# Attention, mixture of experts and feed-forward on one core: the weighted sum of a pair of heads as one group

## The chip, the cores and the metric

The kernel runs on one core of a Trainium2 chip. The metric is the device time of one execution in microseconds. PE is the matrix engine, DVE, ACT and POOL are the vector, scalar and general engines, SP issues most DMAs. PE writes to eight banks of PSUM; DVE and ACT copy from there.

## The reference

Causal attention over 4 batches of 8 heads, 576 queries and keys, head size 64, with a bias from a cumulative sum of `s`; then a top-1 mixture of 8 experts (512 to 1024 to 512) with two gates; then a feed-forward layer 512 to 2048 to 512 with a squared ReLU. Only the attention is touched by the change:

```
scores = scale * np.matmul(q, k.transpose(0, 1, 3, 2))
bias = -(cum[:, :, :, None] - cum[:, :, None, :])
scores = np.where(causal, -1000000000.0, scores + np.minimum(bias, 0.0))
scores = scores - np.max(scores, axis=-1, keepdims=True)
attn = np.exp(scores)
attn = attn / (np.sum(attn, axis=-1, keepdims=True) + 1e-09)
return np.matmul(attn, v)
```

## The kernel before

The attention works on 16 pairs of heads, one pair after the other, and the pairs overlap. The 576 queries are four blocks of 128 and a last one of 64, the last rows. A pair has seven units: blocks 0 and 1 with both heads in one unit, blocks 2 and 3 once for each head (unit 2, 3 and, for the other head, 10, 11), and the last rows of both heads (unit 4). The order within a pair is 0, 1, 3, 11, 2, 10, 4.

For a unit PE computes scores (`emit_s`, L636), DVE adds the mask and takes the row maximum (`emit_m`, L663), ACT takes the exp and its row sum (`emit_e`, L680), PE transposes the result (`emit_t`, L696), and ACT or DVE copies it out (`emit_v`, L715 and L717) into `pt0` (queries of blocks 0 and 1) or `pt1` (the others). From these and v PE makes the weighted sum (`emit_pv`, L733): the first half, 256 queries, in eight rows of the trace, the second half, 320 queries, in twenty. ACT copies it to `oT` (`emit_ov`, L744). PE transposes that back (`emit_xt`, L771), DVE divides by the row sums (`emit_xe`, L806), whose reciprocals are made by `emit_rc` (L759 to L762), and `store_x` sends it to memory. Beside that, q and k of a later pair are transposed by PE (`qk_pe`, L549: four blocks of q, four of k; L551: the last rows of both), split by ACT into a high part (`qk_hi`, L576) and by DVE into a low part (`qk_lo`, L580). For each batch the gate's logits are made from `oT` (`emit_lm`, L828).

The order on each engine is written out by hand: every step is registered by `at(key, function)`, the keys come from the table `K_`, and one sort by key gives the program's order. A pair counts as seven units of key.

PSUM holds three banks "s" for scores, three banks "t" for the transposes of a pair, of q and k, and for the weighted sums, and a pair of banks "s2" for the scores of the last rows. In the banks "t" a pair has thirteen groups: eight of its units (the last rows take two), three of q and k, and the two halves of the weighted sum. The first half of the sum stands early in the next pair's time, the second about five units later.

Of the kernel before, what the change touches and what calls it, by code (L numbers as in the profile page):

```python
# [24 lines left out]
P = 128  # L25
# [17 lines left out]
    lt=[[-0.37, -0.33, 0.07, 0.12], [-0.22, 0.14, 0.64, 0.96]],  # L43
# [12 lines left out]
    qk=[-3.45, -2.16, -1.89],  # L56
    qkh=0.61,
# [3 lines left out]
    pv=[[3.74, 3.87], [8.47, 8.49, 8.51, 8.53, 8.57]],  # L61
# [6 lines left out]
    sx=2.42,  # L68
# [22 lines left out]
def attention_moe_ffn_kernel(  # L91
# [125 lines left out]
    def at(key, fn, *args):  # L217
        tasks.append((key, len(tasks), fn, args))
# [232 lines left out]
    with tc.manual_schedule():  # L451
        with ExitStack() as actx:
# [34 lines left out]
            pt0 = [apool.tile([P, 2, 2, 256], F32, name=f"pt0{a}") for a in range(K_["ptb"])]  # L487
# [13 lines left out]

            raw_q = {}
# [40 lines left out]

            def qk_pe(pp, part):
# [154 lines left out]
            def emit_v(pp, u, act):  # L699
                pb = pp % K_["ptb"]  # L700
                j0 = 0
                for i, (tp, n) in enumerate(t_t.pop((pp, u))):
                    if u < 2:
                        src = tp[:, 0:n * P].rearrange("p (h j i) -> p h j i", h=2, i=P)
                        dst = pt0[pb][:, :, 0:u + 1, u * P:(u + 1) * P]
# [15 lines left out]
            def emit_pv(pp, half, jbs):  # L721
                vt = raw_v[pp]
                if jbs[0] == 0:
                    o_t[pp, half] = ps_o.tile([P, 512], F32, tag=o_tag, name=o_tag)
                o = o_t[pp, half]
                last = 1 if half == 0 else NB - 1
                pt = (pt0 if half == 0 else pt1)[pp % K_["ptb"]]
                n = 256 if half == 0 else S - 256
                base = 0 if half == 0 else 2
                for jb in jbs:  # L730
                    c0 = max(jb - base, 0) * P
                    for hd in range(2):
# [3 lines left out]
                            rhs=pt[:, hd, jb, c0:n],  # L736
# [15 lines left out]
            def emit_rc(pp, half):  # L752
# [4 lines left out]
                b0, b1 = (0, 2) if half == 0 else (2, NB)  # L757
# [476 lines left out]
            order = K_["order"]  # L1234
            NU = len(order)
            at(NU * ND + 0.5, init_spare)

            def early(pp):
                return min(NU, 3 * max(pp - ND, 0))

            for pp in range(NPAIR):
# [5 lines left out]
                if pp >= 1:  # L1247
# [4 lines left out]
                    for part in range(3):  # L1252
                        tq = t0 + K_["qk"][part] - early(pp) + (0 if pp >= ND else K_["q1"])
                        at(tq, qk_pe, pp, part)
                        at(tq + K_["qkh"], qk_hi, pp, part)
                        at(tq + K_["qkl"], qk_lo, pp, part)
                if pp >= ND:
                    tb = t0 + max(K_["dup"], K_["qk"][2] + K_["qkl"] - early(pp) + 0.4)
# [14 lines left out]
                for half in (1, 0) if end else (0, 1):  # L1273
# [5 lines left out]
                    at(tv + K_["rc"], emit_rc, pp, half)  # L1279
# [544 lines left out]
```

## Time and profile before

| what | value |
|---|---|
| median of 3 runs | 861.82 us (861.45 to 862.03) |
| the profiled execution's own time | 862.74 us |
| its span | 861.0 us |
| granted clock of PE in it | 0.998 |
| PE busy | 843.1 us (98%) |
| weight loads of PE busy | 748.7 us (87%) |
| DVE, ACT, POOL busy | 520.4, 452.3, 262.1 us |
| weighted sums (L733) on the chain of waits | 5% of the span |

The span is from the first to the last instruction. Busy time is the union of an engine's instructions, with modelled ends on PE. The chain of waits is followed back from the last instruction, at each step to what released it. The attention takes the first 222 us of the span; the experts and the feed-forward layer, which the change does not touch, follow.

### The profile page before, as it was taken

Reading aid. Unit: us, or ns where it says so; the run is one execution under the profiler, and the core shown is the slowest. Engines: PE = TensorE matmul, PEld = TensorE weight load, DVE = VectorE, ACT = ScalarE, POOL = GpSimd, SP = SyncE. Lnnn points to the kernel's source line nnn. Section 1 sums busy time; section 2 is a strip of 40 time slices with the busy share of each in tenths; the row PEclk is TensorE's granted clock in tenths of the full one; section 3 lists DMA queues with packets and bytes.
Section 4 is the critical chain, followed back from the end, with each engine's and each line's share of the span. In section 5 each row is a group of like instructions: output and inputs, shape, how many; then the busy total and the mean of one; then the engine's idle time right before and its main releaser. Section 6 shows DMA issues by size and latency. Waiting matters only on the chain.

```text
span 861.0 us, 15161 instructions
## 1 busy us (share of the span) xinstructions
PE 843.1 (98%) x5412; PEld 748.7 (87%) x5412; DVE 520.4 (60%) x1180; ACT 452.3 (53%) x1012; POOL 262.1 (30%) x304
## 2 busy tenths in 40 slices
PE   8999999999999999999999999999999999999995
PEld 6876777777799999999999999999999999999994
DVE  7667777978777677768976767664233343232221
ACT  7787878988465446566655545443233232233221
POOL 6322334543126465566422232331101011001001
PEclk9999999999999999999999999999999999999999
DMA  7676677753287898999983433321010121001001
GB/s 168 137 162 142 144 183 180 178 127 91 78 278 232 255 252 266 233 280 274 296 246 96 147 120 101 100 84 62 13 62 37 37 75 38 1 1 37 1 0 40
DMA packets 113029, 113.14 MB, mean 131 GB/s; under 512 B 66034, under 2 KB 83954, under 8 KB 112947
## 3 DMA queue, kind: packets, MB, share of 16 engines
q1 hardware_dynamic: 104962, 96.68, 42.1%
q0 software_dynamic: 3664, 9.62, 3.3%
q10 hardware_dynamic: 4320, 5.80, 2.0%
q8 instruction: 45, 0.74, 0.4%
q14 instruction: 38, 0.30, 0.1%
HBM read 80.50 MB, written 23.32 MB: 121 GB/s over the span
## 4 chain that ended last, share of the span: by engine, by line
PE 47%; issue 31%; DVE 6%; ACT 6%; POOL 5%; DMA 4%; POOLq 1%; SPq 0%; ACTq 0%; DVEq 0%
PE z L1431 14%; PE z L1482 7%; PE z L1473 6%; PE s L636 5%; PE t L733 5%; PE t L696 4%; DMA cv<-in_moe_w_out_dram 2%; ACT p L680 2%; POOL out_dram L1541 1%; DVE w L250 1%; POOL cvm L1400 1%; PE t L549 1%; POOL cvm L1399 1%; ACT sta L576 1%; DMA w_out_d<-cvm 1%
## 5 line engine op out<-in xcount | busy, mean ns | idle before, releaser
L1431 PE MATMUL z<-xt,w 128*128 128x384 f32 (+6 forms) x1920 | 329.7, 320 | 0.7 <-DVE h L1442 0.6
L1431 PEld LDWEIGHTS z<-xt,w 128*128 128x128 f32 x1920 | 308.1, 188 | 9.8 <-DVE h L1442 1.2
L1482 PE MATMUL z<-w,h 128*128 128x512 f32 x864 | 214.9, 393 | 0.0
L1482 PEld LDWEIGHTS z<-w,h 128*128 128x128 f32 x864 | 160.7, 188 | 29.3
L1451 DVE SCALAR_TENSOR_TENSOR r<-z,r 128x384 f32<-128x384 f32 x96 | 53.3, 556 | 127.2 <-ACT r L1450 127.2
L1450 ACT ACTIVATE r<-z 128x384 f32<-128x384 f32 x96 | 47.2, 492 | 150.3 <-PE z L1431 149.3
L1473 PE MATMUL z<-h,w 128*128 128x304 f32 (+5 forms) x768 | 111.3, 294 | 0.4 <-DVE h L1442 0.2
L1473 PEld LDWEIGHTS z<-h,w 128*128 128x128 f32 x768 | 104.0, 189 | 1.2 <-ACT h L1441 0.4
L1399 POOL TENSOR_TENSOR cvm<-cvm,cva 128x512 f32<-128x512 f32 x32 | 43.5, 1361 | 170.6 <-DVE cva L1395 121.9
L1541 POOL DMA_INDIRECT out_dram<-ysb,tok_m x18 | 17.4, 969 | 245.5 <-ACT ysb L1528 183.2
L1458 DVE TENSOR_TENSOR h<-r,h 128x384 fp32r<-128x384 f32 x96 | 61.0, 636 | 50.3 <-ACT h L1457 49.7
L680 ACT ACTIVATE p<-p,nm 128x128 f32<-128x128 f32 (+3 forms) x144 | 84.3, 590 | 3.7 <-DVE nm L663 2.3
L1457 ACT CAST h<-r 128x384 fp32r<-128x384 f32 x96 | 49.3, 513 | 64.1 <-DVE r L1451 63.8
L250 DVE TENSOR_TENSOR w<-stg,w 128x1024 fp32r<-128x1024 f32 x49 | 75.1, 1534 | 5.4 <-ACT w L246 5.4
L663 DVE CUSTOM_DVE_ANT_0 p<-s,mask 128x128 f32<-128x128 f32 (+3 forms) x128 | 59.7, 486 | 30.4 <-PE s L636 29.3
L696 PE MATMUL t<-ident,p 128*128 128x128 f32 x400 | 69.1, 283 | 2.8 <-DVE sta L580 1.1
L246 ACT CAST w<-stg 128x1024 fp32r<-128x1024 f32 x49 | 51.4, 1049 | 22.0 <-POOL cvm L1400 18.2
L696 PEld LDWEIGHTS t<-ident,p 128*128 128x128 f32 x400 | 44.4, 140 | 18.7 <-ACT p L680 6.2
L597 POOL CAST stb<-sta 64x1152 fp32r<-64x1152 f32 x28 | 31.4, 1150 | 79.7 <-PE s L636 46.3
L1400 POOL TENSOR_TENSOR cvm<-cvs,cvm 128x512 f32<-128x512 f32 x32 | 54.2, 1694 | 2.5
L636 PE MATMUL s<-sta 128*64 128x288 f32 (+4 forms) x204 | 50.0, 342 | 0.9 <-DVE sta L580 0.9
L715 ACT COPY pt<-t 128x512 f32<-128x512 f32 (+1 forms) x94 | 47.0, 515 | 7.3 <-PE t L733 4.1
(242 smaller groups left out, 1024.8 us busy)
## 6 DMA issues: line engine op xcount, KB each, us to landing
stg<-in_moe_w_dram SPq DMA_DIRECT2D x42, 512.0 KB
cv<-in_moe_w_out_dram SPq DMA_DIRECT2D x16, 512.0 KB
stx<-in_moe_w_dram SPq DMA_DIRECT2D x14, 512.0 KB
cv<-in_moe_w_in_dram SPq DMA_DIRECT2D x14, 512.0 KB
xr<-yT_d SPq DMA_DIRECT2D x8, 768.0 KB
qk<-in_q_dram SPq DMA_DIRECT2D x32, 128.0 KB
v<-in_v_dram SPq DMA_DIRECT2D x32, 128.0 KB
stg<-in_moe_w_dram SPq DMA_DIRECT2D x16, 256.0 KB
```

Source lines behind the costliest of these rows:

```text
L250: nc.vector.tensor_tensor(out=lo, in0=raw.pop(job), in1=hi.bitcast(F32), op=ALU.subtract)
L636: nc.tensor.matmul(ps[0:mw, d0:d0 + nn], lhsT=ql[r, m0:m0 + mw], rhs=kl[r, c0:c0 + nn], start=(i == 0 and (tail or n == 0)), stop=(done an ...
L663: nc.vector.tensor_tensor_reduce(out=dst, in0=src, in1=msk, scale=-1.0, scalar=3.0e38, op0=ALU.add, op1=ALU.min, accum_out=nm[:, c:c + 1])
L680: nc.scalar.activation(out=pt[:, cs], in_=pt[:, cs], func=AF.Exp, scale=-1.0, bias=nm[:, c:c + 1], accum_out=rs[:, r:r + 1])
L696: nc.tensor.transpose(tp[:, i * P:(i + 1) * P], pt[:, j0:j0 + P], ident)
L1399: nc.gpsimd.tensor_tensor(out=m, in0=m, in1=a.bitcast(F32), op=ALU.mult)
L1400: nc.gpsimd.tensor_tensor(out=m, in0=sq, in1=m, op=ALU.add)
L1431: nc.tensor.matmul(ps[:, 0:n], lhsT=wa[:, zw, kk, fl * P:(fl + 1) * P], rhs=xt[:, zx, kk, 0:n], start=(i == 0), stop=(i == 3 * KD - 1))
L1451: nc.vector.scalar_tensor_tensor(out=gg, in0=ps[:, 0:TT], scalar=0.0, in1=gg, op0=ALU.max, op1=ALU.mult)
L1458: nc.vector.tensor_tensor(out=ht[:, 1], in0=gg, in1=ht[:, 0].bitcast(F32), op=ALU.subtract)
L1473: nc.tensor.matmul(y_acc[g][d][:, 0:n], lhsT=wb[:, zw, fl, d * P:(d + 1) * P], rhs=ht[:, zh, 0:n], start=(f == 0 and i == 0), stop=(f == n ...
L1482: nc.tensor.matmul(acc, lhsT=ht[:, zh, c * P:(c + 1) * P], rhs=wb[:, zw, fl, :], start=(first and i == 0), stop=(last and i == 2))
```

## The change

For pairs 0 to 14 the two halves of the weighted sum stand together, where the second half stood, in one buffer of the bank pair "s2"; ACT copies them out one after the other. The eight transposes of q and k (pairs 2 and 4 to 15; not 3) become one group in another buffer of "s2", behind the scores of the next pair's block 0. The pair of banks has one buffer, so it is used in turn: last rows' scores, q and k, weighted sum, last rows' scores. `pt0` is kept twice, in a layout where each block of keys is contiguous. The reciprocals of both halves are made at once, the first half's division and the store come later. One key moves the first group of logits next to the second. Pair 15 keeps its own arrangement.

```diff
-    lt=[[-0.37, -0.33, 0.07, 0.12], [-0.22, 0.14, 0.64, 0.96]],
+    lt=[[-0.37, -0.33, 0.07, 0.12], [-0.36, 0.14, 0.64, 0.96]],
...
+    qk2=[-2.05, -2.04, -1.59],
+    qkd=[-0.25, 0.54, 0.0],
...
-    pv=[[3.74, 3.87], [8.47, 8.49, 8.51, 8.53, 8.57]],
+    x0=10.87,
+    pv=[[8.45, 8.46], [8.47, 8.49, 8.51, 8.53, 8.57]],
...
-    sx=2.42,
+    sx=3.9,
...
-            pt0 = [apool.tile([P, 2, 2, 256], F32, name=f"pt0{a}") for a in range(K_["ptb"])]
+            pt0 = [apool.tile([P, 2, 3 * P], F32, name=f"pt0{a}") for a in range(2)]
...
+            def in_s2(pp):
+                return pp >= ND and early(pp) != 3
+
             def qk_pe(pp, part):
-                ps = qk_ps[pp, part] = bank(K_["ring"][part])
+                if part < 2 and in_s2(pp):
+                    if part == 0:
+                        qk_ps[pp] = ps_2.tile([P, 1024], F32, tag="s2", name="s2")
+                    ps = qk_ps[pp][:, 512 * part:512 * part + 512]
+                else:
+                    ps = bank(K_["ring"][part])
+                qk_ps[pp, part] = ps
...
                 if jbs[0] == 0:
-                    o_t[pp, half] = ps_o.tile([P, 512], F32, tag=o_tag, name=o_tag)
+                    if pp == NPAIR - 1:
+                        o_t[pp, half] = ps_o.tile([P, 512], F32, tag=o_tag, name=o_tag)
+                    else:
+                        if half == 0:
+                            o_t[pp] = ps_2.tile([P, 1024], F32, tag="s2", name="s2")
+                        o_t[pp, half] = o_t[pp][:, 512 * half:512 * half + 512]
...
                     for part in range(3):
-                        tq = t0 + K_["qk"][part] - early(pp) + (0 if pp >= ND else K_["q1"])
+                        tq = t0 + K_["qk2" if in_s2(pp) else "qk"][part] - early(pp) + (0 if pp >= ND else K_["q1"])
                         at(tq, qk_pe, pp, part)
-                        at(tq + K_["qkh"], qk_hi, pp, part)
-                        at(tq + K_["qkl"], qk_lo, pp, part)
+                        th = K_["qkd"][part] if in_s2(pp) else 0.0
+                        at(tq + th + K_["qkh"], qk_hi, pp, part)
+                        at(tq + th + K_["qkl"], qk_lo, pp, part)
...
-                    at(tv + K_["rc"], emit_rc, pp, half)
+                    if end or half == 1:
+                        at(tv + K_["rc"], emit_rc, pp, half)
+                    if not end and half == 0:
+                        tv = tv - K_["pv"][0][-1] + K_["x0"]
+                        tx = tv + K_["xe"]
                     at(tv + K_["xt"], emit_xt, pp, half)
```

The order of PE from the last rows' scores of one pair to the transposes of its unit 10, in the next pair's time, before (`s_865` is the bank pair, `pt_154` is `pt0`):

```order
L636 MATMUL s_865<-stb_138 128x288 x4
L636 MATMUL s_865<-sta_137 64x288 x4
L549 MATMUL t<-ident,qk 128x128 x4
L733 MATMUL t<-pt_154,v_142 64x256 x2
L733 MATMUL t<-pt_154,v_142 64x128 x2
L696 MATMUL t<-ident,p 128x128 x3
L636 MATMUL s<-sta_135 128x192 x2
L636 MATMUL s<-stb_139 128x192 x2
L549 MATMUL t<-ident,qk 128x128 x4
L771 MATMUL s<-ident,oTx 128x128 x2
L696 MATMUL t<-ident,p 128x128 x3
```

The same stretch of PE in the changed kernel, where lines below L549 are moved by some 17 to 25 (L653 is the scores, L713 the transposes, L566 q and k, L796 the x transposes; `s_901` is the bank pair again):

```order
L653 MATMUL s_854<-stb_138 128x288 x4
L653 MATMUL s_854<-sta_137 64x288 x4
L713 MATMUL t<-ident,p 128x128 x3
L653 MATMUL s<-sta_135 128x192 x2
L653 MATMUL s<-stb_139 128x192 x2
L796 MATMUL s<-ident,oT_310 128x128 x2
L566 MATMUL s_901<-ident,qk 128x128 x8
L713 MATMUL t<-ident,p 128x128 x3
L653 MATMUL s<-sta_135 128x256 x2
```

The first half of the sum (two rows on `pt_154`) is gone from here, q and k have become one row behind block 0's scores and the x transposes, and block 2's transposes follow the last rows' scores at once.

The place of the second half of the sum on PE, before (`pt_155` is `pt1`):

```order
L696 MATMUL t<-ident,p 128x128 x4
L636 MATMUL s<-sta_135 128x384 x2
L733 MATMUL t<-pt_155,v_142 64x320 x6
L733 MATMUL t<-pt_155,v_142 64x192 x2
L733 MATMUL t<-pt_155,v_142 64x64 x2
L696 MATMUL t<-ident,p 128x128 x4
L636 MATMUL s<-stb_139 128x384 x2
```

And in the changed kernel (L758 is the sum, `s_978` the bank pair):

```order
L713 MATMUL t<-ident,p 128x128 x4
L653 MATMUL s<-sta_135 128x384 x2
L758 MATMUL s_978<-pt_154,v_142 64x256 x2
L758 MATMUL s_978<-pt_154,v_142 64x128 x2
L758 MATMUL s_978<-pt_156,v_142 64x320 x6
L758 MATMUL s_978<-pt_156,v_142 64x192 x2
L758 MATMUL s_978<-pt_156,v_142 64x64 x2
L713 MATMUL t<-ident,p 128x128 x4
L653 MATMUL s<-stb_139 128x384 x2
```

Two rows on `pt_154` now stand ahead of those on `pt1`, into the same buffer.

The order of ACT over the same time, from the high part of q to the exps of block 1, before (L744 is the copy of the first half of the sum, L715 copies transposes):

```order
L576 ACTIVATE sta_137<-t 128x512
L744 COPY oTx<-t 128x256
L680 ACTIVATE p,rs_156<-p,nm 128x576
L576 ACTIVATE sta_137<-t 128x512
L715 COPY pt_155<-t 128x3x128
L576 ACTIVATE sta_137<-t 128x2x64
L680 ACTIVATE p,rs_157<-p,nm 128x128 x2
L715 COPY pt_155<-t 128x2x3x64
L715 COPY pt_155<-t 128x2x2x64
L680 ACTIVATE p,rs_157<-p,nm 128x256 x2
```

And in the changed kernel (L697 is the exp, L593 the high parts, L732 the copies, `s_901` is the bank pair):

```order
L697 ACTIVATE p,rs_157<-p,nm 128x576
L593 ACTIVATE sta_137<-s_901 128x512
L732 COPY pt_156<-t 128x3x128
L697 ACTIVATE p,rs_158<-p,nm 128x128 x2
L593 ACTIVATE sta_137<-t 128x2x64
L593 ACTIVATE sta_137<-s_901 128x512
L732 COPY pt_156<-t 128x2x3x64
L732 COPY pt_156<-t 128x2x2x64
L697 ACTIVATE p,rs_158<-p,nm 128x256 x2
```

The exp of the last rows (128x576) now stands first, the copy of the sum is gone, and the high part of k (the second L593 on `s_901`) stands behind block 0's exps and the high part of the last rows.

## Rows read from the trace of the kernel before

**Rows 1.** Chain of waits, the attention: start us, length us, what.

```profile
31.42 2.21 PE t L733 x20
...
45.72 2.21 PE t L733 x20
...
57.75 2.21 PE t L733 x20
69.78 2.21 PE t L733 x20
...
95.94 2.21 PE t L733 x20
108.52 2.21 PE t L733 x20
...
208.66 2.21 PE t L733 x20
```

**Rows 2.** Busy time by stretch: window, us, busy PE PEld DVE ACT POOL, PE clock, DMA, GB/s.

```profile
49.39:190.06 140.67, 138.02 (x1110) 104.32 (x1108) 109.15 (x387) 117.35 (x341) 53.14 (x68) 1.00 0.68 158
```

**Rows 3.** Timeline of PE: start us, us, instruction [idle before <- what ended it].

```profile
61.42 0.78 PE L636 MATMUL s<-stb 128*128 128x288 f32 x4
...
62.56 0.60 PE L549 MATMUL t<-ident,qk 128*128 128x128 f32 x4
63.09 0.87 PE L733 MATMUL t<-pt,v 128*64 128x256 f32 x8
63.89 0.55 PE L696 MATMUL t<-ident,p 128*128 128x128 f32 x3
...
64.71 0.60 PE L549 MATMUL t<-ident,qk 128*128 128x128 f32 x4
65.14 0.38 PE L771 MATMUL s<-ident,oTx 128*128 128x128 f32 x2
...
68.50 0.92 PE L696 MATMUL t<-ident,p 128*128 128x128 f32 x4 [0.15 <-ACT p L680]
```

**Rows 4.** Timeline of ACT, the same lap.

```profile
60.00 0.43 ACT L744 COPY oTx<-t 128x320 f32<-128x320 f32 x1 [1.21 <-PE t L733]
...
63.20 0.60 ACT L576 ACTIVATE sta<-t 128x512 fp32r<-128x512 f32 x1 [0.30 <-PE t L549]
64.01 0.37 ACT L744 COPY oTx<-t 128x256 f32<-128x256 f32 x1 [0.21 <-PE t L733]
64.28 0.78 ACT L680 ACTIVATE p<-p,nm 128x576 f32<-128x576 f32 x1
...
65.39 0.60 ACT L576 ACTIVATE sta<-t 128x512 fp32r<-128x512 f32 x1 [0.24 <-POOL sta L598]
65.89 0.48 ACT L715 COPY pt<-t 128x384 f32<-128x384 f32 x1
...
68.33 0.52 ACT L680 ACTIVATE p<-p,nm 128x256 f32<-128x256 f32 x1
...
68.82 0.72 ACT L680 ACTIVATE p<-p,nm 128x512 f32<-128x512 f32 x1
...
69.53 0.59 ACT L715 COPY pt<-t 128x512 f32<-128x512 f32 x1
```

**Rows 5.** Timeline of DVE, the same lap.

```profile
63.55 0.08 DVE L663 DVE_READ_ACCUMULATOR2_ANT nm<- 128x1 f32 x1
```

**Rows 6.** Timeline of PE, first lap.

```profile
43.28 0.30 PE L551 MATMUL t<-ident,qk 128*128 128x128 f32 x1 [0.78 <-issue]
```

**Rows 7.** Waits of PE, 49.39 to 190.06: us in total, times, longest.

```profile
PE t L696 <- DVE sta L580: 1.1, 2, 0.7
```

**Rows 8.** Timeline of DVE, a lap with the gating's work.

```profile
100.20 0.31 DVE L945 TENSOR_SCALAR r<-iota_r,rk_all 128x384 bf16<-128x384 f16 x1
...
100.72 1.16 DVE L945 TENSOR_SCALAR r<-iota_r,rk_all 128x384 bf16<-128x384 f16 x1
```

**Rows 9.** Timeline of POOL, the same lap.

```profile
100.62 2.27 POOL L597 CAST stb<-sta 64x1152 fp32r<-64x1152 f32 x2 [5.69 <-ACT pt L715]
```

More of the change, by code (lines that the diff above doesn't have):

```diff
@@ L500, in warm @@
                     nc.tensor.matmul(wt[:, 0:w], lhsT=onesb, rhs=onesb.unsqueeze(1).to_broadcast([P, w // P, P]), start=True, stop=True)
+            order = K_["order"]
+            NU = len(order)
             raw_q = {}
@@ L542, in attention_moe_ffn_kernel, with early @@
             qk_ps = {}
+            def early(pp):
+                return min(NU, 3 * max(pp - ND, 0))
+            def in_s2(pp):
+                return pp >= ND and early(pp) != 3
             def qk_pe(pp, part):
-                ps = qk_ps[pp, part] = bank(K_["ring"][part])
+                if part < 2 and in_s2(pp):
[5 more added lines that the diff above has]
+                qk_ps[pp, part] = ps
                 if part < 2:
@@ L703, in emit_v @@
                     if u < 2:
-                        src = tp[:, 0:n * P].rearrange("p (h j i) -> p h j i", h=2, i=P)
-                        dst = pt0[pb][:, :, 0:u + 1, u * P:(u + 1) * P]
+                        src = tp[:, 0:n * P].rearrange("p (h c) -> p h c", h=2)
+                        dst = pt0[pp % 2][:, :, u * P:(2 * u + 1) * P]
                     elif u == NB - 1:
@@ L723, in emit_pv @@
                 if jbs[0] == 0:
-                    o_t[pp, half] = ps_o.tile([P, 512], F32, tag=o_tag, name=o_tag)
+                    if pp == NPAIR - 1:
[4 more added lines that the diff above has]
+                        o_t[pp, half] = o_t[pp][:, 512 * half:512 * half + 512]
                 o = o_t[pp, half]
                 last = 1 if half == 0 else NB - 1
-                pt = (pt0 if half == 0 else pt1)[pp % K_["ptb"]]
                 n = 256 if half == 0 else S - 256
@@ L731, in emit_pv @@
                     c0 = max(jb - base, 0) * P
+                    if half == 0:
+                        pt = pt0[pp % 2][:, :, 2 * c0:n + c0]
+                    else:
+                        pt = pt1[pp % K_["ptb"]][:, :, jb, c0:n]
                     for hd in range(2):
@@ L735, in emit_pv @@
                             lhsT=vt[:, jb, hd, :],
-                            rhs=pt[:, hd, jb, c0:n],
+                            rhs=pt[:, hd],
                             start=(jb == 0), stop=(jb == last))
@@ L756, in emit_rc @@
                 rsv = rs.rearrange("p (h t) -> p h t", h=2)
-                b0, b1 = (0, 2) if half == 0 else (2, NB)
+                b0, b1 = (0, 2) if half == 0 else (2 if pp == NPAIR - 1 else 0, NB)
                 if half == 1:
@@ L1232, in attention_moe_ffn_kernel @@
             new_half(wpool1, (0, "b"), "w1")
-            order = K_["order"]
-            NU = len(order)
             at(NU * ND + 0.5, init_spare)
-            def early(pp):
-                return min(NU, 3 * max(pp - ND, 0))
             for pp in range(NPAIR):
@@ L1252, in attention_moe_ffn_kernel @@
                     for part in range(3):
[L1253 removed]
+                        tq = t0 + K_["qk2" if in_s2(pp) else "qk"][part] - early(pp) + (0 if pp >= ND else K_["q1"])
                         at(tq, qk_pe, pp, part)
[L1255 to L1256 removed]
+                        th = K_["qkd"][part] if in_s2(pp) else 0.0
+                        at(tq + th + K_["qkh"], qk_hi, pp, part)
+                        at(tq + th + K_["qkl"], qk_lo, pp, part)
                 if pp >= ND:
[L1258 removed]
+                    tb = t0 + max(K_["dup"], K_["qk2" if in_s2(pp) else "qk"][2] + K_["qkl"] - early(pp) + 0.4)
                     at(tb - 0.05, load_aug, pp, 1)
```

## The prediction

> **What bounds the kernel now.** I read the chain of waits first. Through the attention it goes from one second-half weighted sum to the next, one a pair [rows 1]: 31.42, 45.72, 57.75, 69.78 and so on to 208.66, fifteen rows and fourteen laps between them. The last pair and the gating follow in the same chain, so I take what a lap gains or loses to reach the end undiminished. The laps are of five kinds. The first is 14.30 us (31.42 to 45.72). Five are plain, 12.03 (57.75 to 69.78). Three carry the logits of a batch and are some 2 us longer. Three carry other work of the gating on DVE and are a little over half a microsecond longer, as 95.94 to 108.52, 12.58. The last two are shorter. Before the first sum lies pair 0.
>
> Second came the busy times by stretch. From 49.39 to 190.06 us PE is busy 138.02 of 140.67 us, its weight loads 104.32, DVE 109.15, ACT 117.35 [rows 2]. By the first number PE alone is the bound and the first rival below is right; but the ends of matmuls are modelled, so I go by the order of events in a lap. The Trainium skill, Perfetto Trace Analysis, Identifying the Most-Contended Engine, calls matmul occupancy a poor measure for TensorE and weight-load occupancy a better one; by that rule, 104.32 of 140.67 or 74%, PE has room and a plain lap is bound elsewhere, by the other number the change would bring the first rival's time.
>
> Third, one 12.03 us lap instruction by instruction, on PE [rows 3] and ACT [rows 4]. The reader is to see a loop: the last rows' scores start on PE at 61.42 and end where q's transposes begin, 62.56; DVE takes their row maximum, which is read out from 63.55 [rows 5] for 0.08, so at 63.63; then ACT runs without a real pause from 63.20 to the second exp of block 1 at 68.33, and PE's transposes of block 1 start at 68.50, released by that exp after an idle 0.15. From there PE goes on by itself (scores of block 2, weighted sum at 69.71, and the next pair's last rows). So the loop has an ACT part of 68.33 − 61.42 = 6.91 us and a PE part behind it. While ACT works through its part PE has other work for nearly all of it, so the two are close.
>
> **The change, part by part.** Durations are from the profiled execution, 862.74 us with a span of 861.0, 0.92 above the runs' median of 861.82; the sum is a difference, and I add it to either.
>
> *The weighted sum of the first half, moved.* It stands at 63.09 and takes 0.80 to the next group; the second half takes 2.21 [rows 1, 3]. The first streams 768 columns (2×256 + 2×128), the second 2432 (6×320 + 2×192 + 2×64). Two equations give 1.41/1664 = 0.85 ns a column and 0.15 us a group. So 0.65 us leaves the ACT part of the loop, where PE hides beside ACT, and enters the PE part, where nothing hides it: **+0.65** a lap. The group's own 0.15 goes. So does a change of kind: q's four transposes, behind scores, take 0.53 to the next start and k's four 0.43 [rows 3]; I read 0.10 as the cost of a break. PE's own work falls by 0.25 a pair; that is worth something only where PE bounds.
>
> *ACT's order.* ACT's part now holds the exp of the last rows first, then hi q, the copy of block 2's transposes, block 0's exps, hi of the tail, hi k, the rest. Gone from it is the copy of the first half's sum (64.01 to 64.28: 0.27), which now stands with the second half's, where ACT idled 1.21 us at 60.00, so it costs nothing there. Two waits go as well [rows 4]. Hi q to the copy is 0.81, while the same instruction takes 0.50 at 65.39: 0.31. The tail's exp to hi k is 1.11; by 0.71 for an exp of 512 columns (68.82 to 69.53) it should be about 0.76 for 576: 0.35. The same work back to back is 5.13 − 0.27 − 0.31 − 0.35 = 4.20. It can start when the row maximum is there: 63.63 plus 0.1 for the hand-over (my choice) is 2.32 after the scores' start. I add 0.14 for block 2's copy, since its three transposes now stand behind the group of eight: scores 1.14, block 2's and block 0's work 0.82, the x transposes some 0.2, eight transposes 0.86 with 0.14 waiting for the maximum to free the bank pair, some 0.5 to transpose and hand over, against ACT free at 3.58. Sum 2.32 + 4.20 + 0.14 = 6.66, against 6.91: **−0.25**. At the best the copy of block 2 doesn't wait at all, −0.39; at the worst it waits twice as long, about −0.10.
>
> A 12.03 us lap therefore changes by **+0.65 − 0.25 = +0.40** (0.26 to 0.55). Were PE the bound, it would change by −0.25.
>
> *The group of eight in the bank pair.* Queued behind its wait on PE are block 2's transposes and all scores. PE's own work from the last rows' scores to block 1's transposes is 7.08 − 0.15 − 0.80 − 0.10, about 6.0, against ACT's 6.66 + 0.17; so up to 0.8 us of waiting there costs nothing. The pair's next users: the weighted sum needs lo k done; lo k follows hi k, which stands ahead of the exps of blocks 1 and 3, so it is done long before. The last rows' scores need both copies of the sum, two pieces of 0.4 (60.00 [rows 4]) after it, while 61.42 − 57.75 − 2.21 = 1.46 us of other PE work lies between: 0.6 to spare. I cost these at nothing; without the cover the price is what the second and third rivals say. The Trainium skill, Perfetto Trace Analysis, Matmuls, wants independent groups to rotate through different banks so that copying out one overlaps the next; three groups through one buffer is against it. By that rule each turn would show; by the rows the turns are covered. No bank pair with this turn is in the trace.
>
> *The freed banks.* Of thirteen groups a pair through three banks nine are left. The one large wait for a bank is 0.78 us at 43.28 ahead of q's and k's tail [rows 6], in the 14.30 lap. I take **−0.70**, bounds −1.03 (it and the 0.25) and 0 (another wait in its place). The later ones on lo are 1.1 us in two pieces, 0.7 the longest [rows 7].
>
> *Reciprocals, first half's x, store.* One set of reciprocals less a pair on DVE, just ahead of the last rows' maximum, which waits for PE anyway: nothing in a plain lap. In the laps with other DVE work the second comparison of ranks takes 1.16 us beside a POOL cast begun at 100.62, the first, at 100.20, 0.31 [rows 8, 9]. With the reciprocals gone the second starts ahead of the cast, and up to 0.55 (12.58 − 12.03 [rows 1]) comes back: −0.15 to +0.40 a lap. I take 0, nearer to the lower end, because the saved wait is in the rows. The first half's x transposes and the later store only move; their DMA has a lap to land.
>
> *The logits.* The two groups stand together; I give them the 0.25 that I gave the sum: +0.40 − 0.25 = +0.15 a lap (bounds −0.25 and +0.40).
>
> *The last two laps and pair 0.* The former carry less and lie between −0.25 and +0.40; I take 0. Pair 0 has four passes of scores, PE bounds it: −0.25, bounds −0.25 and +0.40.
>
> **Sum.** 5 × 0.40 = 2.00; 3 × 0.15 = 0.45; 3 × 0 and 2 × 0; −0.70; −0.25. Together **+1.5 us**: 861.8 + 1.5 = 863.3 (of the profiled execution, 864.2). Its own range: the five laps give ±0.75; the other terms' bounds together are −2.5 and +4.1, taken half way since they are independent, −1.2 and +2.0: 861.4 to 866.1.
>
> **Rivals.**
> *PE is the bound, 0.28.* For it: 98% busy, and the idle of 0.15 ahead of block 1's transposes; if the ACT part shrinks by more than I give it, PE's own order sets the lap. Against: the ACT part can shrink only by its pauses, 0.66, and the 0.27 of the copy, and the exp of the last rows can't start before its maximum. Its time: fifteen pairs × 0.25 = 3.75 and 0.78 of the wait, −4.5: **857.3**.
> *Lo of q and k becomes a wait of every lap, slower, 0.17.* Lo of the tail and lo k now stand behind block 1's maxima on DVE, lo of the tail holds one of three transpose banks, and block 0's transposes need it. The row for it is PE waiting on lo, up to 0.7 a time [rows 7]. It decides as soon as lo of the tail ends so late that block 0's transposes, and the scores between them and block 1's, are not done when ACT has finished block 1's second exp. At 0.25 more a lap, about a third of that 0.7, in 13 laps: +1.5 + 3.3 = +4.8, **866.6**. Against: a wait of PE up to the 0.8 above is free.
> *The bank pair's turn, slower, 0.05.* The last rows' scores wait for the sum's copies where ACT starts these behind an exp of 512 columns that isn't done: 0.71 less the 0.6 to spare is 0.1, and as much again for the group of eight, 0.2 a lap in 13: +1.5 + 2.6 = +4.1, **865.9**. ACT's 1.21 us of idle time before the copy speaks against it.
> *It doesn't matter, 0.05.* PE's saving and the longer PE part cancel everywhere: 861.8.
>
> **Chances and range.** The forecast has 0.45. About 0.2%, 1.7 us, is what a measurement of this kernel can tell from no change. The forecast lies just under that, so I split it 0.25 within and 0.20 slower. Faster: 0.28. Within: 0.25 + 0.05 = 0.30. Slower: 0.20 + 0.17 + 0.05 = 0.42. The range reaches from the first rival to the second with a little over: 857.2 to 867.0; the likeliest case alone, 861.4 to 866.1.
>
> **What would show it.** Right: in a plain lap the time from the last rows' scores to block 1's transposes falls from 7.08 to about 6.8, PE idles about 0.8 more before them, and the weighted sum takes 2.86 us in one piece, the lap 12.4. Wrong, if laps fall to 11.8 with no idle of PE (the first rival), if block 0's transposes wait for lo (the second), if the scores of the last rows wait for a copy of the sum (the third), or if the 43.28 wait only changes its name.

## The result: 1.0% slower, and the profile after

| | before | after |
|---|---|---|
| median of 4 runs each | 861.92 us (861.45 to 862.45) | 871.04 us (869.15 to 871.59) |
| ratio, 95% interval | | 1.0102 (1.0084 to 1.0119) |
| span of the profiled execution | 861.0 us | 869.9 us |

The time lies above the predicted range, 857.2 to 867.0. In this text hi and lo are the high and low parts of q and k, and the tail is their last rows. Where the span's 8.9 us arose is read first from the chain of waits, with the same stations as in [rows 1]. The weighted sum is now one row of 28 instructions, whose second half starts 0.65 us behind its start. The chain of the kernel after (start, length, what):

```profile
47.09 2.92 PE s L758 x28
59.81 2.86 PE s L758 x28
72.48 2.86 PE s L758 x28
...
152.02 2.86 PE s L758 x28
165.92 2.86 PE s L758 x28
...
215.04 2.85 PE s L758 x28
226.44 1.83 PE t L758 x20
```

A plain lap is 72.48 − 59.81 = 12.67 where it was 12.03. Compared station by station:

| stretch | forecast | measured | from |
|---|---|---|---|
| up to pair 1's second half | −0.95 | +2.0 | 47.09 + 0.65 against 45.72 |
| five plain laps | +2.00 | +3.0 | 0.69, 0.64, 0.64, 0.53, 0.52 |
| three laps with logits | +0.45 | +0.3 | 0.13, 0.14 and nothing |
| three laps of the gating | 0 | +1.7 | 13.09, 12.69, 13.90 against 12.58, 12.65, 12.75 |
| two short laps | 0 | 0 | −0.28 and +0.31 |
| last pair | 0 | −0.2 | 226.44 − 215.69 against 219.62 − 208.66 |
| behind the attention | no term | +2.1 | 869.9 − 226.44 against 861.0 − 219.62 |
| sum | +1.5 | +8.9 | |

More than half of the loss is in three places that the forecast gave nothing or a gain: the start, the gating laps, and a stretch that the change does not touch.

**The plain lap.** The timeline of PE, kernel after, the lap that answers to [rows 3] (start, length, instruction, idle before it and what ended that):

```profile
59.74 2.92 PE L758 MATMUL s<-pt,v 128*64 128x256 f32 x28
...
64.21 0.78 PE L653 MATMUL s<-stb 128*128 128x288 f32 x4
...
66.49 1.09 PE L566 MATMUL s<-ident,qk 128*128 128x128 f32 x8
69.94 0.44 PE L713 MATMUL t<-ident,p 128*128 128x128 f32 x2 [0.39 <-DVE sta L597]
...
71.20 0.92 PE L713 MATMUL t<-ident,p 128*128 128x128 f32 x4 [0.35 <-ACT p L697]
...
72.41 2.93 PE L758 MATMUL s<-pt,v 128*64 128x256 f32 x28
```

I cut the lap as the prediction did. From the last rows' scores to block 1's transposes: 71.20 − 64.21 = 6.99 (before 7.08, forecast 6.83). From there to the sum 1.21, as before. From the sum to the next scores 64.21 − 59.74 = 4.47 (before 3.74, forecast +0.65; the sum of [rows 1] at 57.75 stands at 57.68 in the timeline, as 59.81 here at 59.74). PE idles 0.35 for the exp, not the expected 0.8, and 0.39 ahead of block 0's transposes for lo of the tail, which is the sign that the second rival named. ACT's side, as [rows 4]:

```profile
66.47 0.78 ACT L697 ACTIVATE p<-p,nm 128x576 f32<-128x576 f32 x1 [0.79 <-DVE nm L680]
...
67.62 0.60 ACT L593 ACTIVATE sta<-s 128x512 fp32r<-128x512 f32 x1 [0.28 <-PE s L566]
```

The exp of the last rows starts 2.26 after the scores, as reckoned (2.32), and hi of q behind it waits another 0.28: it starts 0.04 after the row of all eight transposes ends (66.49 + 1.09 = 67.58), not when q's four do.

**Pair 1.** Before, the first half's sum stood between pair 1's last rows and the block-0 scores of pair 2. Without it PE comes there early. PE of the kernel after, from these scores to pair 1's sum:

```profile
38.75 0.33 PE L653 MATMUL s<-sta 128*128 128x192 f32 x1 [1.61 <-DMA sta<-aug_d]
39.29 0.36 PE L653 MATMUL s<-sta 128*128 128x192 f32 x1 [0.22 <-DMA sta<-sta]
39.49 0.44 PE L653 MATMUL s<-stb 128*128 128x192 f32 x2
...
41.65 1.74 PE L566 MATMUL s<-ident,qk 128*128 128x128 f32 x8
...
47.09 2.92 PE L758 MATMUL s<-pt,v 128*64 128x256 f32 x28 [0.59 <-DVE sta L597]
```

PE waits 1.61 and 0.22 us for pair 2's operands, which a transfer brings. That wait only takes back what the moved sum and an earlier start (below) had won. In the kernel before, PE passes the same point at 39.66, so here, at 39.49, it is still 0.17 ahead:

```profile
39.66 0.39 PE L636 MATMUL s<-stb 128*128 128x192 f32 x2
```

From there to the sum it takes 47.09 − 39.49 = 7.60 us, in the kernel before 45.65 − 39.66 = 5.99 (to the second half; its start in the timeline). The rows are longer: the eight transposes of pair 4's q and k take 1.74, in the plain lap 1.09. The windows of the same stretch (us, busy PE PEld DVE ACT POOL, granted clock, DMA share, GB/s):

```profile
40.90:43.20 2.30, 2.30 (x13) 2.30 (x13) 0.78 (x4) 1.25 (x5) 0.00 (x0) 0.53 0.97 197
43.20:47.00 3.80, 3.25 (x20) 2.05 (x18) 2.25 (x6) 3.57 (x12) 0.00 (x0) 1.00 0.81 195
```

The granted clock is 0.53 from 40.90 to 43.20, the lower of its two levels (1.2 GHz), and 1.00 again from 43.20. Before, from 39.40 to 43.20, it was 1.00:

```profile
39.40:43.20 3.80, 3.10 (x29) 2.86 (x26) 3.12 (x12) 3.60 (x12) 1.35 (x3) 1.00 0.57 141
```

Last in this stretch the sum waits 0.59 for the low part of q and k, which still holds the bank pair. So the +2.0 is about 1.6 of slower rows and the 0.65 of the moved sum, less the 0.17. a_p2 below makes the 1.6 a price of the clock.

**A gating lap.** Waits of PE from 51 to 208 us, kernel after (us in total, times, longest), against [rows 7]:

```profile
PE t L713 <- DVE sta L597: 9.1, 11, 2.0
```

The longest, 2.0, is in the lap 152.02 to 165.92. DVE first, then POOL, ACT and PE in it:

```profile
158.56 1.12 DVE L970 TENSOR_SCALAR r<-iota_r,rk_all 128x384 bf16<-128x384 f16 x1
...
160.49 1.20 DVE L970 TENSOR_SCALAR r<-iota_r,rk_all 128x384 bf16<-128x384 f16 x1
...
161.95 0.67 DVE L597 SCALAR_TENSOR_TENSOR sta<-s,sta 128x512 fp32r<-128x512 f32 x1
```

```profile
157.33 2.23 POOL L614 CAST stb<-sta 64x1152 fp32r<-64x1152 f32 x2 [3.83 <-PE s L653]
...
160.29 1.28 POOL L276 TENSOR_TENSOR w<-stg,w 128x512 fp32r<-128x512 f32 x1
```

```profile
162.65 0.60 ACT L593 ACTIVATE sta<-s 128x512 fp32r<-128x512 f32 x1 [0.92 <-DVE sta L597]
```

```profile
163.79 0.44 PE L713 MATMUL t<-ident,p 128*128 128x128 f32 x2 [2.03 <-DVE sta L597]
```

The comparisons of ranks (L970) stand at 158.56 and 160.49, each while POOL works, and take 1.12 and 1.20 instead of the 0.31 of [rows 8]. Lo of q (161.95) stands behind both. ACT's hi of k waits for it, lo of the tail comes still later on DVE, and PE waits 2.03 for that. But slow comparisons are not new here: in the kernel before the five of this lap take 0.31, 1.07, 0.53, 0.60 and 0.31, together 2.82, and in the kernel after 3.17, while the lap grew by 1.15. Their new place counts for more than their length; how much of the 1.15 is theirs, this trace alone does not show.

**Behind the attention.** The first group of expert matmuls follows the last of the early matmuls (L1124, before L1099). PE before, PE after, ACT after:

```profile
236.08 1.17 PE L1099 MATMUL z<-w,sta 128*128 128x512 f32 x4
237.08 1.50 PE L1431 MATMUL z<-xt,w 128*128 128x224 f32 x12
```

```profile
244.11 1.17 PE L1124 MATMUL z<-w,sta 128*128 128x512 f32 x4
246.46 1.60 PE L1456 MATMUL z<-xt,w 128*128 128x224 f32 x12 [1.18 <-ACT xt L1366]
```

```profile
245.44 0.97 ACT L1366 CAST xt<-z 128x512 fp32r<-128x512 f32 x2 [6.05 <-PE z L1124]
```

The gap is 2.35 instead of 1.00: the copy that feeds the experts waits until the early matmuls are done. The diff touches neither of them. What differs is where the buffers behind `pt0` lie; b_pt0 and a_mem below test that.

### The profile page after: what moved, and what is told of

Same layout as the page of the kernel before. It is cut to its first block, busy times and chain, and to the rows that moved or that the text cites. A ratio compares the mean times of both kernels' runs of the same rounds, so it can differ in the third digit from the quotient of the medians.

```text
span 869.9 us, 15109 instructions
## 1 busy us (share of the span) xinstructions
PE 839.6 (97%) x5412; PEld 747.8 (86%) x5412; DVE 513.2 (59%) x1150; ACT 449.8 (52%) x1012; POOL 262.8 (30%) x304
## 4 chain that ended last, share of the span: by engine, by line
PE 51%; issue 30%; ACT 6%; DVE 4%; POOL 4%; DMA 3%; POOLq 1%; SPq 1%; ACTq 0%; DVEq 0%
PE z L1456 17%; PE z L1498 9%; PE z L1507 7%; PE s L758 5%; PE s L653 4%; PE t L713 3%; ACT p L697 2%; PE s L566 1%; POOL out_dram L1566 1%; ACT pt L732 1%; ACT sta L593 1%; DMA cv<-in_moe_w_out_dram 1%; PE s L796 1%; PE z L336 1%; DVE p L680 1%
## 5 line engine op out<-in xcount | busy, mean ns | idle before, releaser
L697 ACT ACTIVATE p<-p,nm 128x128 f32<-128x128 f32 (+3 forms) x144 | 85.1, 597 | 11.1 <-DVE nm L680 10.7
L713 PE MATMUL t<-ident,p 128*128 128x128 f32 x400 | 67.3, 282 | 12.5 <-DVE sta L597 9.1
L713 PEld LDWEIGHTS t<-ident,p 128*128 128x128 f32 x400 | 45.1, 141 | 27.1 <-DVE sta L597 13.9
L653 PE MATMUL s<-sta 128*64 128x288 f32 (+4 forms) x204 | 49.7, 339 | 2.9 <-DMA sta<-aug_d 1.6
L732 ACT COPY pt<-t 128x512 f32<-128x512 f32 (+1 forms) x94 | 47.1, 520 | 7.3 <-PE t L758 2.5
```

The costliest lines, as they stand in the source:

```text
L653: nc.tensor.matmul(ps[0:mw, d0:d0 + nn], lhsT=ql[r, m0:m0 + mw], rhs=kl[r, c0:c0 + nn], start=(i == 0 and (tail or n == 0)), stop=(done an ...
L697: nc.scalar.activation(out=pt[:, cs], in_=pt[:, cs], func=AF.Exp, scale=-1.0, bias=nm[:, c:c + 1], accum_out=rs[:, r:r + 1])
L713: nc.tensor.transpose(tp[:, i * P:(i + 1) * P], pt[:, j0:j0 + P], ident)
```

## The experiments

"Ratio" is against the kernel before on the same chip; "pair 2" is the start of its last rows' scores, "lap" the next one, a plain one, "gating" the lap of pair 10 counted from last rows' scores, "gap" the one from the last early matmul to the experts.

| kernel | median us | ratio (95%) | pair 2 | lap | gating | gap |
|---|---|---|---|---|---|---|
| before | 861.92 | | 49.39 | 12.03 | 12.74 | 1.00 |
| after | 871.04 | 1.0102 (1.0084–1.0119) | 51.55 | 12.66 | 13.89 | 2.35 |
| b_pt0 | 863.15 | 1.0015 (1.0006–1.0025) | 50.10 | 12.03 | 12.76 | 2.35 |
| b_eight | 866.15 | 1.0055 (1.0038–1.0072) | 48.42 | 12.68 | 13.19 | 1.01 |
| a_noeight | 869.86 | 1.0100 (1.0071–1.0128) | 51.15 | 12.12 | 13.46 | 2.36 |
| a_p2 | 870.03 | 1.0088 (1.0072–1.0105) | 49.82 | 12.67 | 15.51 | 2.36 |
| a_split | 874.52 | 1.0142 (1.0124–1.0160) | 52.23 | 12.99 | 15.30 | 2.36 |
| a_hiq | 874.38 | 1.0157 (1.0141–1.0174) | 49.38 | 12.89 | 15.42 | 2.35 |
| a_lo2 | 869.61 | 1.0087 (1.0072–1.0102) | 50.16 | 12.66 | 13.70 | 2.36 |
| a_mem | 868.55 | 1.0078 (1.0062–1.0093) | 51.38 | 12.67 | 13.90 | 1.02 |
| v1 | 863.28 | 1.0030 (1.0018–1.0043) | 49.95 | 12.12 | 12.83 | 1.02 |
| v2 | 863.53 | 1.0031 (1.0019–1.0042) | 49.74 | 12.11 | 12.80 | 1.02 |
| v3 | 867.97 | 1.0074 (1.0060–1.0088) | 53.27 | 12.11 | 13.71 | 1.02 |
| v4 | 863.45 | 1.0028 (1.0016–1.0040) | 49.51 | 12.14 | 12.86 | 1.01 |

**b_pt0**: the kernel before with nothing but `pt0` kept twice in the new layout.

```diff
-            pt0 = [apool.tile([P, 2, 2, 256], F32, name=f"pt0{a}") for a in range(K_["ptb"])]
+            pt0 = [apool.tile([P, 2, 3 * P], F32, name=f"pt0{a}") for a in range(2)]
...
```

> The kernel before with pt0 alone changed: two buffers in the contiguous layout (6 KB a partition in place of 4 KB), every order as before. Theory (the 2.1 us that the changed kernel loses behind the attention come from where the later buffers lie in memory, so that the first gather and the first copies of the experts wait for other readers): about 864.0 us, the attention's chain as before (last pair's sum at 219.6), the loss between 228 and 245 us. Rival (the loss comes from the later stores or from chance): 861.9 within 0.5.

All laps from pair 2 on are those of before, and the gap is there, 2.35. ACT of b_pt0:

```profile
238.74 0.97 ACT L1344 CAST xt<-z 128x512 fp32r<-128x512 f32 x2 [5.47 <-PE z L1102]
```

ACT waits 5.47 us for the same early matmuls. The gap comes with the new `pt0`, and no sum has to move for it. The whole stretch behind the attention is only 0.7 longer than before, 862.4 − 220.32 = 642.1 us against 641.4, not the expected 2.1.

**b_eight**: the kernel before with the eight transposes as one group in the bank pair; the sums stay.

```diff
+    qk2=[-2.05, -2.04, -1.59],
+    qkd=[-0.25, 0.54, 0.0],
...
+                if part < 2 and in_s2(pp):
+                    if part == 0:
+                        qk_ps[pp] = ps_2.tile([P, 1024], F32, tag="s2", name="s2")
...
```

> The kernel before with q's and k's transposes alone as a group of eight in the bank pair, the weighted sums as before. Theory (the lap grows by the 0.65 us of the moved sum and by little else): plain laps 11.9 to 12.1, the second pair's scores still wait some 1 to 1.5 us for the copy of pair 2's operands, laps with the gating's work 0.3 to 0.8 longer; 863 to 865 us. Rival (the turn of the bank pair is what costs): plain laps 12.5 and more, above 868.

PE of b_eight in a plain lap:

```profile
48.42 0.78 PE L652 MATMUL s<-stb 128*128 128x288 f32 x4
...
56.15 0.93 PE L712 MATMUL t<-ident,p 128*128 128x128 f32 x4 [0.36 <-ACT p L696]
...
57.36 2.27 PE L749 MATMUL t<-pt,v 128*64 128x320 f32 x20
...
61.10 0.78 PE L652 MATMUL s<-stb 128*128 128x288 f32 x4
```

and ACT:

```profile
52.56 0.60 ACT L592 ACTIVATE sta<-s 128x512 fp32r<-128x512 f32 x1 [0.85 <-PE s L565]
```

Scores to block 1's transposes 7.73, sum to scores 3.74 as before (61.10 − 57.36, the sum's start): the group of eight alone makes the lap 0.65 longer, and all of it in the ACT part. In the kernel before hi of q stood ahead of the last rows' exp, in the time in which ACT waits for the maximum [rows 4]; now it stands behind the exp and waits there too, 0.85. My theory, that the group of eight adds little, fell; the rival had the lap right (12.5 and more) and the time too high. Pair 2 starts 0.97 earlier than before, 0.29 of it because pair 0's last rows do (19.93 against 20.22): the laps of pairs 0 and 1 are 0.68 shorter, and here the freed banks pay what was forecast, 0.70, although only two of the four groups have left them.

**a_noeight**: the kernel after without the group of eight.

```diff
             def in_s2(pp):
-                return pp >= ND and early(pp) != 3
+                return False
```

> The changed kernel with q's and k's transposes as before (two groups of four in the three banks, at their old places), the weighted sum still one group in the bank pair. Theory: plain laps 12.4 to 12.7 from the sum alone, no wait of pair 2's scores for a transfer, 2.1 us behind the attention: 866.5 to 868.5. Rival (the eight is the cause): 862 to 864.

```profile
51.15 0.77 PE L653 MATMUL s<-stb 128*128 128x288 f32 x4
...
57.62 0.89 PE L713 MATMUL t<-ident,p 128*128 128x128 f32 x4
...
58.80 2.93 PE L758 MATMUL s<-pt,v 128*64 128x256 f32 x28
...
63.27 0.78 PE L653 MATMUL s<-stb 128*128 128x288 f32 x4
```

Scores to block 1's transposes 6.47, sum to scores 4.47, the lap 12.12. So the moved sum adds 0.73 to one part and takes 0.61 from the other. In this lap the two parts of the change add up: 7.08 − 0.61 + 0.65 = 7.12 against the measured 6.99. Over all laps they do not (us against the kernel before, from the chains of waits):

| laps | the eight alone (b_eight) | the sum alone (a_noeight) | both (after) |
|---|---|---|---|
| five plain | +3.5 | +0.8 | +3.0 |
| three with logits | +1.8 | +1.0 | +0.3 |
| three of the gating | +0.6 | +2.1 | +1.7 |

"The sum alone" takes with it its reciprocals, division, store and the new `pt0`, which by b_pt0 changes no lap. The plain laps are the eight's and the gating laps the moved sum's. The kernel is still 1.0% slower, above both what I expected and what the rival gave. Its loss is at the start, where PE waits 2.44 us and the clock falls (first PE, then the window):

```profile
39.04 0.56 PE L653 MATMUL s<-sta 128*128 128x192 f32 x2 [2.44 <-DMA sta<-aug_d]
```

```profile
39.00:42.60 3.60, 3.56 (x18) 3.59 (x18) 1.53 (x6) 1.21 (x3) 0.00 (x0) 0.53 0.66 136
```

and in the gating laps and the gap.

**a_p2**: the kernel after with q and k of pair 2 transposed as before, in two groups of four in pair 0's lap (21.55 and 23.19 us). The group of eight in pair 1's lap, that of pair 4, stays.

```diff
-                return pp >= ND and early(pp) != 3
+                return pp > ND and early(pp) != 3
```

> The changed kernel with pair 2's q and k alone transposed as before. Theory (pair 2's operands are made up to 3 us later than before and their copy by DMA is no longer hidden): the wait of 1.6 us for sta and the slow rows behind it go, 871.0 - 2.5 = 868.5. Rival (the wait only moves to the bank pair's turn behind it): 870.5 to 871.5.

Pair 2 starts 1.7 earlier than in the kernel after, and the clock stays at 1.00:

```profile
39.09 0.44 PE L653 MATMUL s<-sta 128*128 128x192 f32 x2 [1.70 <-POOL oTx L1252]
39.37 0.39 PE L653 MATMUL s<-stb 128*128 128x192 f32 x2
...
45.35 2.92 PE L758 MATMUL s<-pt,v 128*64 128x256 f32 x28 [0.59 <-DVE sta L597]
...
164.63 4.03 PE L758 MATMUL s<-pt,v 128*64 128x256 f32 x28
```

```profile
39.00:42.60 3.60, 3.51 (x29) 3.31 (x29) 1.90 (x10) 2.16 (x8) 0.54 (x2) 1.00 0.81 167
```

The idle time of 1.70 is about as long as in the kernel after, so against the theory the wait did not go (nor did the time fall to 868.5), and the wait alone does not settle the clock. From the same point to the sum, with the same work on PE and the same 0.59 for lo, it is 45.35 − 39.37 = 5.98 us here and 7.60 in the kernel after: the lower clock cost 1.62. What was won was lost in the lap of pair 10, 15.51 against 13.89, again 1.62, and again with the clock:

```profile
164.00:166.00 2.00, 2.00 (x13) 1.18 (x13) 1.90 (x7) 1.68 (x5) 2.00 (x5) 0.50 0.82 201
```

The comparisons (1.13 and 1.21) and PE's wait for lo (2.04, up to 162.08) are there as in the kernel after, but the sum that follows takes 4.03, not 2.93. In the kernel after the clock stays at 1.00 behind a wait of 2.03. a_split and a_hiq lose in this lap in the same way (15.30 and 15.42, with 0.50 to 0.65 granted in the two stretches of 2 us in which it is lowest).

**a_split and a_hiq**: the group of eight parted: unit 10's transposes stand between q's four and k's, in a_hiq the scores behind them too, and there hi of q is issued ahead of k's four. First a_split, then a_hiq:

```diff
-    qk2=[-2.05, -2.04, -1.59],
-    qkd=[-0.25, 0.54, 0.0],
+    qk2=[-2.05, -1.95, -1.59],
+    qkd=[-0.25, 0.45, 0.0],
```

```diff
-    qk2=[-2.05, -2.04, -1.59],
-    qkd=[-0.25, 0.54, 0.0],
+    qk2=[-2.05, -1.80, -1.59],
+    qkd=[-0.60, 0.30, 0.0],
```

> The changed kernel with the group of eight parted: q's four transposes, then block 2's three, then k's four, into the same two banks. Theory (the first copy of q waits until all eight transposes are done, and stands at the head of ACT's part of the loop): that copy starts 0.3 to 0.4 us earlier behind the last rows' scores, plain laps fall from 12.67 to 12.25-12.4, 13 laps: 866.5 to 868. Rival (the late place of the eight, behind the scores of block 0 and the maximum, is the cost, however it is parted): plain laps 12.55 to 12.7, 870 to 871.

> The changed kernel with the eight parted once more, but q's high part issued ahead of k's transposes, which stand behind the scores of block 1. Theory (ACT's copy of q's half of the bank pair waits for the last transpose issued into the pair before it, be it q's or k's): the copy now starts as soon as the exp of the last rows is done, 0.4 to 0.7 us earlier, plain laps 12.2 to 12.45 (12.67 and 12.99 with the eight whole and parted), 866 to 868.5. Rival (the exp of the last rows and the late start of q's transposes set it, not that wait): 12.6 and more.

ACT of a_split, then PE of a_hiq:

```profile
55.96 0.60 ACT L593 ACTIVATE sta<-s 128x512 fp32r<-128x512 f32 x1 [0.61 <-PE s L566]
```

```profile
53.83 0.66 PE L566 MATMUL s<-ident,qk 128*128 128x128 f32 x4 [0.71 <-DVE sta L597]
```

In a_split the row of q's transposes ends at 55.16 and hi of q starts at 55.96, just behind k's four (55.32 + 0.60 = 55.92): it waited for both. In a_hiq hi of q goes at once, and k's transposes wait 0.71 until DVE has read q's half. So the halves of the bank pair exclude each other in both directions; they are used as one buffer. Neither order helps: the plain laps are 12.99 and 12.89, and both were slower than the kernel after. I had expected both to be faster.

**a_lo2**: the low part of the tail ahead of block 1's maxima on DVE.

```diff
-    qk2=[-2.05, -2.04, -1.59],
+    qk2=[-2.05, -2.04, -1.86],
```

> The changed kernel with q's and k's last rows transposed 0.27 of a unit earlier, so that their low part stands ahead of block 1's row maxima on DVE, not behind them. Theory (in the laps with the gating's work PE's transposes of block 0 wait up to 2.0 us for a bank that this low part holds): those waits fall under 0.5 us, the laps of pairs 9 and 10 from 12.69 and 13.89 to at most 12.6 and 13.0, the plain laps unchanged within 0.1: 869.5 to 870.2. Rival (DVE is late there for other reasons): the laps keep their length, 871.

The lap of pair 10 falls from 13.89 to 13.70 only. Its PE:

```profile
161.34 0.41 PE L713 MATMUL t<-ident,p 128*128 128x128 f32 x2 [1.20 <-DVE sta L597]
```

PE's wait falls from 2.03 to 1.20 and the lap by 0.19, so the place of the tail's lo is not what makes it long. Lo of q still stands behind the slow comparison (1.20 us from 158.87, lo of q at 160.33). This theory fell.

**a_mem**: the kernel after with the two `pt0` put where later buffers keep their old addresses.

```diff
-            pt0 = [apool.tile([P, 2, 3 * P], F32, name=f"pt0{a}") for a in range(2)]
+            pt0 = [apool.tile([P, 2, 4 * P], F32, name="pt00")]
...
+            pt0_p = actx.enter_context(tc.tile_pool(name="pt0", bufs=1))
+            pt0.append(pt0_p.tile([P, 2, 3 * P], F32, name="pt01"))
```

> The changed kernel with the second pt0 in a pool behind all others and the first in a slot of the old size, so that every other buffer of the attention lies where it lay before. Theory (the larger pt0 moves the attention's buffers, and the experts' first copy then waits for the matmuls that read what lies under it): that copy follows its transposes again at once, the experts' first matmul starts 1.0 us after the last early matmul, not 2.35; 869 to 869.7, the attention unchanged. Rival (the wait belongs to the order of the changed kernel): 2.35 stays and the time with it, 871.

```profile
243.88 1.18 PE L1124 MATMUL z<-w,sta 128*128 128x512 f32 x4
244.90 1.27 PE L1458 MATMUL z<-xt,w 128*128 128x224 f32 x10
```

The gap is 1.02 again, and from the last sum of the chain to the end of the span it is 641.4 us (867.7 − 226.28), as before (861.0 − 219.62), where the kernel after has 643.5. Laps are unchanged. This settles the gap, 1.35 of the +2.1: all seven kernels with the moved buffers have 2.35 or 2.36, and all seven with the old addresses 1.00 to 1.02. The rest is not settled. From the last sum to the last early matmul a_mem is as late as the kernel after (17.6 us and 17.7, before 16.5), and what follows the gap varies from one profiled execution to the next (622.8 in a_mem, 623.4 after, 623.9 before).

**v1 to v4**: attempts at a better version: no group of eight, old addresses, both halves of the sum in the bank pair and copied together, the first half at four places, with one `pt0`. The diff is that of v1; v2, v3 and v4 have 4.85, 7.3 and 5.2 for 4.2. The lines for one `pt0` and for q and k as before are left out.

```diff
-    pv=[[8.45, 8.46], [8.47, 8.49, 8.51, 8.53, 8.57]],
+    pv=[[4.2, 4.21], [8.47, 8.49, 8.51, 8.53, 8.57]],
...
-                    at(tv + K_["ov"], emit_ov, pp, half, K_["ovact"][half])
+                    at((tv if end or half else base + 8.46) + K_["ov"], emit_ov, pp, half, K_["ovact"][half])
```

> A version that may beat both: both halves of the sum in the bank pair and copied together as in the changed kernel, but the first half made early, behind the next pair's scores of block 0, where PE has time beside ACT; q and k as before; one pt0 in the old memory. Theory (the part of the loop on PE must not grow, and ACT's part is shorter without the copy and its waits): plain laps 11.7 to 11.95, 857.5 to 860.5. Rival (the lap is set by PE's own work, which is unchanged): plain laps 12.0, 861 to 862.5. The theory that the turn of the bank pair costs wherever it stands: 864 and more.

> As v1, with the first half of the sum behind k's transposes, not ahead of them. In v1's plain lap of 12.12 ACT waits 0.84 us for k's transposes, which stand behind the first half. Theory (the loop through ACT sets the lap): that wait goes, block 1's transposes come 0.3 to 0.5 earlier, plain laps 11.6 to 11.85, 857 to 860. Rival (PE's own work is the bound): 12.0 to 12.1, 862 to 863.5.

> As v1, with the first half of the sum directly ahead of block 1's transposes, where PE waits for ACT. Theory (the loop through ACT): plain laps 11.6 to 11.85 as in v2, 857 to 860, unless DVE's copy of the next pair's block 0, which now waits for this sum to have read pt0, delays block 3's maximum: then 12.0 and more. Rival (PE's own work is the bound): 12.0 to 12.1, 862 to 863.5.

> As v1, with the first half of the sum behind the scores of block 1, so that neither k's nor block 3's transposes of the pair before, for which ACT waited 0.84 and 0.97 us in v1 and v2, stand behind it; behind it stand the last rows' transposes. Theory (a lap of 12.1 in v1, v2 and v3 is each time a wait of ACT or of a transpose bank, not PE's own work): plain laps 11.8 to 12.0, 859.5 to 862. Rival (PE's own work with its bank waits gives 12.1 wherever the first half stands): 12.1, 863 to 864.

None beats the kernel before; the best are 0.3% slower. The plain lap is 12.1 wherever the first half stands. All four theories fell, and the rival in each, that PE's own work sets the lap, had the lap about right (12.0 to 12.1). v3, with the first half ahead of block 1's transposes, comes to pair 2 3.9 us later, at the lower clock too (0.50 to 0.52 from 40 to 46 us), and has gating laps of 13.5 to 13.7, so a late first half is bad at both places. Why the lap does not fall below 12.03 when PE has a group less to do stays open: in a_noeight ACT has no pause over 0.18 from the exp on, in v1 it pauses 0.84 up to the end of k's transposes, and the lap is the same. PE as the bound, the first rival, is not refuted for these laps.

## Why the prediction was wrong

*The direction was right, and the loop for the plain lap.* In four of the five plain laps of the kernel after, PE's last wait is the one for block 1's exp (0.35 to 0.39), at the end of the loop of scores, maximum, ACT's chain and block 1's transposes. The two parts changed by +0.73 and −0.09 where +0.65 and −0.25 were forecast. That mis-sizing is worth 0.24 in this lap and 1.0 us over the five. One slip is in the working: the sum for block 2's copy gives 1.14 + 0.82 + 0.2 + 0.86 + 0.14 + 0.5 = 3.66 against 3.58, so 0.08 and not the 0.14 that was added, and it has no wait ahead of hi of q, where 0.28 was measured.

*What causes it was wrong.* "I cost these at nothing", of the group of eight. Alone it costs 0.65 a plain lap (b_eight), and the moved sum, to which I charged the +0.40, costs 0.09 alone in the same lap (a_noeight) and 0.8 us over the five. The step's error: it asked whether PE's waiting is covered, and took hi of q's new place, behind the exp, as ACT work without a pause. In the kernel before hi of q used the time in which ACT waits for the maximum. Parting the eight only moves the wait, since the two halves exclude each other: 0.61 of ACT in a_split, 0.71 of PE in a_hiq. The Trainium skill, Perfetto Trace Analysis, Matmuls, which the prediction set against the rows, asks that independent groups rotate through different PSUM banks so that copying one out overlaps the next one's matmuls. Here, where q and k share one buffer, they did not overlap: in a_hiq k's transposes waited 0.71 us until q's half was read.

*"The freed banks", −0.70, and pair 0, −0.25.* The stretch lost 2.0 instead. In b_eight, where the sum stays, the first term comes out (0.68). In the kernel after PE does run ahead, but its gain ends at the wait for pair 2's operands (1.61 and 0.22), behind which it is only 0.17 ahead of the kernel before. The 0.78 us wait is gone, and 0.59 of waiting for lo stands in its place: it mostly changed its name, which the prediction gave as a sign of being wrong. The moved sum's 0.65, charged to every plain lap, was not charged to this stretch, and the lower clock costs 1.6. The prediction had no term for the clock. Nor does the wait come from the moved sum alone. The profiled executions reach pair 0's last rows at times between 18.54 and 20.22 us, the kernel after at 19.23, before at 20.22. b_pt0, also at 19.23 and with the sum in its place, waits 0.91 and 0.32 for the same operands, and keeps the full clock. It reaches pair 2 at 50.10, the kernel after at 51.55, so against it 1.45 us are the change's. What decides whether the clock falls stays open: behind single idle times of 1.70 (a_p2) and 1.83 (a_lo2) it stayed at 1.00, behind 1.91 (a_mem) and 2.44 (a_noeight) it fell, and in the gating lap it fell behind 2.04 (a_p2) and not behind 2.03 (after).

*The gating laps, 0.* +1.7 was measured; the bound given was +0.40 a lap, and one lap has +1.15. The reciprocals that left DVE were to let the second comparison go ahead of POOL's cast, and it does (two in 0.54 from 156.92, the cast from 157.33). But the third and the fourth then meet POOL's work (1.12 and 1.20 for 0.31), the fourth just ahead of lo of q, and lo of q and of the tail behind it hold up ACT and PE. By a_noeight, +2.1 without the group of eight, it is the moved sum with what goes along that lengthens these laps; by which step is not isolated.

*The second rival, 0.17,* was nearer than the forecast allowed. Its sign came: from 51 to 208 us PE waits for lo once in each of eleven laps, 0.35 to 2.03, 9.1 us in all against 1.1, and 4.3 of it in the three gating laps. In seven of the eleven no wait for the exp follows, so there lo came last. Its price, 0.25 a lap, was too small. The size of a gating lap varies with order and clock, from 12.83 (v1) to 15.51 (a_p2) for pair 10.

*The doubled `pt0`.* The prediction gave it no term. It moves the buffers behind it, and by b_pt0 and a_mem that is 1.35 us of the 2.1 that the stretch behind the attention lost. An allocation can be read from the diff; it should have been a term.

*The logits*, +0.45, came out at +0.3, the last two laps at nothing, as forecast, and the last pair at −0.2. That the logits came out is partly luck, since each half of the change alone costs more there (+1.8 and +1.0).

*The range* failed since three stretches left their bounds: the start (at most +0.40 was allowed, +2.0 measured), the gating laps (+1.2 and +1.7), and the stretch behind the attention, which had no term. With the start at zero and the 2.1 and the gating's 1.7 added, the forecast's own +1.5 would have been about +6.3.

## What to carry to other kernels

Before a piece of work is moved, ask what stands behind it: a transfer that shows no wait in any row can be a microsecond from showing one (b_pt0, 1.0 earlier than the kernel before, waits 1.23), and a gain ahead of it is lost there; the distance from the transfer's landing to its first reader tells. Split a loss into the wait and what follows it: here the wait cost nothing against the kernel before, and the slower rows behind it cost 1.6 us. An instruction that stands in an engine's unavoidable wait is free there and costs its full length one place later. When a buffer grows, everything allocated behind it moves, and a stretch that the diff does not touch can pay; try the new allocation alone first.

## What was not expected of the hardware

- The granted clock was 0.53 for 2.3 us behind the wait at the start of the kernel after and for 3.6 us in a_noeight, and 1.00 in a_p2 and a_lo2 behind nearly the same idle time. In the lap of pair 10 it fell to 0.50 in a_p2 behind 2.04 and stayed at 1.00 in the kernel after behind 2.03. Where it fell, it cost 1.62 us both times that it can be priced.
- A comparison of ranks on DVE took 0.31 us alone, and 1.12 to 1.20 while POOL worked, beside a cast (2.23) as beside an operation on weights (1.28).
- The two banks of one pair did not behave as two buffers: readers of one half waited for writers of the other (0.61 in a_split) and writers for readers (0.71 in a_hiq). Whether the chip or the program's own semaphores cause that, no run here tells.
